# Moving one weight-load issue behind two casts on GpSimd's queue in a retention and Fourier-mixing kernel

## The chip, the cores and the metric

The kernel runs on one core of a Trainium2 chip. The metric is the device time of one execution in microseconds (us). The kernel before was run three times (233.35, 234.04 and 234.59 us), with a median of 234.04 us. One execution was recorded by the hardware profiler; it took 233.47 us, of which the profile's span covers 231.6 us.

A core has TensorE (PE, matrix products), VectorE (DVE), ScalarE (ACT), GpSimd (POOL) and SyncE (SP), each working through its own queue of instructions in order, and 16 DMA engines that serve all transfers. A transfer is issued by an instruction in some engine's queue. In this kernel the loads of q, k and v are issued by SyncE, those of the weights by GpSimd.

## What is computed

Four batches, eight heads, 768 positions, head width 64. First a retention layer, a recurrence over positions with one decay factor for each head:

```python
gamma = 1.0 - 2.0 ** (-5.0 - np.arange(H))
for t in range(S):
    state = gamma * state + einsum('bhd,bhe->bhde', k[:, :, t], v[:, :, t])
    y[:, :, t] = D ** -0.5 * einsum('bhd,bhde->bhe', q[:, :, t], state)
x = y.transpose(0, 2, 1, 3).reshape(B, S, H * D)
```

Then a Fourier mixing, a normalisation and a feed-forward layer of width 2048, each with the sum around it:

```python
u = x + real(fft(fft(x, axis=1), axis=2))
un = (u - mean(u)) / sqrt(var(u) + 1e-6)
out = u + maximum(un @ w_ch1, 0.0) @ w_ch2
```

## The kernel before

**Tiles.** The 768 positions are cut into six chunks of 128, the eight heads into four pairs. Within a chunk the retention is a masked product of q and k, applied to v; across chunks a state for each pair is carried forward. The Fourier transforms are products with tables of sines and cosines that the kernel makes at its start. The feed-forward layer works on blocks of 128 hidden columns.

**The first batch** has a schedule written out by hand: the string FIRST (lines 36 to 48) is a list of units, and each unit's instructions are pinned, on every engine that it uses, behind those of the unit before (the function pin, line 165). A unit's name has a kind, its indices, and behind the @ the engine (v VectorE, a ScalarE, g GpSimd). So the list sets for each engine the order of its queue; units of different engines wait for each other only where data or a buffer make them. The later batches follow a second list, LATER, in the same manner.

**The units around the change**, all of the first batch; the first index is the pair in the order of loading, 0 to 3:

- q3 (line 512): GpSimd's cast of the last pair's q to 16 bits.
- k30 and k31 (line 520, instructions at L528 and L530): cast of the last pair's k, scaled by a decay for each position, one head each, the first on ScalarE and the second on GpSimd.
- v21 and v22 (line 534, L542 and L545): cast of the third pair's v, chunks 0 to 2 on GpSimd, chunks 3 to 5 on ScalarE.
- t30, t31 (L559): TensorE's transposes of the last pair's q and k; e30, e31 (L568, L571): ScalarE's copies of them out of the accumulator memory.
- am30, am31 (L585): the products of q and k; ae.. (L599): their masks on VectorE.
- kv2 (L613): TensorE's products of k and v of the third pair, one for each chunk but the last.
- gk2 (L317): GpSimd's copy of the third pair's decay factors into one of two buffers.
- sc2 (L622): VectorE's scan over the chunks, which reads the products of kv2 and the factors of gk2 and writes the states s.
- yi20, yi21 (L635) and yx2 (L645): TensorE's two parts of the third pair's y, within the chunk and from the states; x20, x21 (L659, L662) scale and store them.
- fs.. (L806) and s... (L873): the first fold and the first Fourier products.
- w0 to w3 (w1_unit, L1363): issue of one quarter of the first FFN weight each; w4 to w7 (w2_unit, L1370) the same for the second. Such a transfer also turns the numbers from 32 to 16 bits. All eight are issued by GpSimd.

**The loads behind them.** SyncE issues all of the first batch's loads and two q loads of the second batch at the start. The next loads (load_unit, L246) wait until the seventh weight transfer (w6) has landed and until one product of the first batch's feed-forward layer (i13, L1184) is done.

Of the kernel before, what the change touches and what calls it, by code (L numbers as in the profile page):

```python
# [37 lines left out]
ts1 ta00 e01@a ta10 ta22 v00@g par@v q1 gk0@g k10@v k11@a ta12 am00 am01 fill3 ta42 ta11 k20@g  # L38
ae010@v ae001@v kv0 ae000@v ae011@v t10 sc0 t11 e10@a yi01 v10@g yi00 yx0 e11@a fill1 am10 q2
x01@a am11 ts3 ta32 ta20 x00@v ta01 fl4@g ae101@v ae100@v k21@a kv1 fill1 t20 ta21 e20@a ae111@v  # L40
yi11 t21 sc1 ae110@v yi10 fs0 fl2@g yx1 q3 s110 w0 k31@g e21@a x10@v am20 am21 x11@a fs1 ta40
v22@a s010 k30@a t30 e30@a t31 v21@g e31@a ae201@v ta30 ae200@v kv2 ae211@v yi21 ae210@v gk2@g
sc2 csn2@a w1 csn1@v am30 ae300@v ta31 yi20 yx2 v32@g x20@a ae301@v xs0@v x21@a ta41 fl3@a gk3@g
s100 am31 ae311@v s000 v31@g kv3 fs2 s101 ge10@a ae310@v w2 s001 w3 yi31 sc3 ge00@a yi30 yx3 g0
x30@a sa00 sa10 edge x31@v fs3 w4 gr0 sa11 csn0@v s011 xs2@a xs3@v w5 s111 xs1@a sa20 mean
# [1457 lines left out]
```

## Time and profile before

| what | value |
|---|---|
| median of three runs | 234.04 us |
| the profiled execution | 233.47 us |
| its span | 231.6 us |
| granted TensorE clock | 0.998 of full speed |
| bytes moved | 36.84 MB |
| weight transfers | 8, 512 KB each |
| median from issue to landing of a weight transfer | 10.8 us |

A row of the timeline has the start in us from the span's start, the time it takes, the engine, the line, the operation, output and inputs by the program's names with their shapes, and in brackets how long the engine stood idle before it and what ended that. A row of the chain of waits has start, duration and the work that the end of the program can be followed back to. In the rows of slices each digit is the busy share of one fortieth of the span (5.8 us) in tenths.

### The profile page before, as it was taken

How to read it: one execution, taken by the hardware profiler on the slowest of the kernel's cores; microseconds unless marked ns; L12 is line 12 of the kernel's file. 1: busy time of each engine (PE TensorE's matmuls, PEld its weight loads, DVE VectorE, ACT ScalarE, POOL GpSimd, SP SyncE). 2: the span in 40 equal slices, each digit the busy share in tenths (PEclk: the TensorE clock that was granted, in tenths of full speed). 3: DMA queues.
4: the chain of work that ended last, by engine and by line, in shares of the span. 5: the costliest groups of instructions: out<-in, count | busy, mean ns of one | idle time of the engine just before them, and what ended most of it. 6: DMA issues, size and time to landing. Idle time of an engine off the chain costs nothing.

```text
span 231.6 us, 6275 instructions
## 1 busy us (share of the span) xinstructions
PE 219.1 (95%) x2407; PEld 179.2 (77%) x2407; DVE 197.1 (85%) x490; ACT 149.5 (65%) x377; POOL 107.7 (46%) x184
## 2 busy tenths in 40 slices
PE   0888999999999999999999999999999999999993
PEld 0356779866675657988999989989889898888892
DVE  8699987859589999999999699999998977959293
ACT  5989858769998576776947748868517745232510
POOL 8378901756760399948104969832003333520000
PEclk9999999999999999999999999999999999999999
DMA  7999999999999999999998795866102221221202
GB/s 168 239 264 250 238 206 207 203 242 260 168 251 220 215 217 216 223 234 219 217 213 189 161 185 157 161 93 116 23 0 95 48 91 28 62 72 25 91 0 93
DMA packets 100957, 36.84 MB, mean 159 GB/s; under 512 B 91456, under 2 KB 97984, under 8 KB 100928
## 3 DMA queue, kind: packets, MB, share of 16 engines
q1 hardware_dynamic: 96704, 32.25, 68.2%
q0 software_dynamic: 4224, 4.19, 10.9%
q8 instruction: 19, 0.31, 0.6%
q14 instruction: 10, 0.08, 0.1%
HBM read 27.26 MB, written 6.29 MB: 145 GB/s over the span
## 4 chain that ended last, share of the span: by engine, by line
PE 69%; DVE 9%; POOL 6%; issue 6%; DMA 5%; SPq 2%; ACT 1%; DVEq 0%; POOLq 0%; ACTq 0%
PE psh L1259 24%; PE ps L1308 21%; PE psc L1206 4%; PE psh L1184 4%; DMA v<-in_v_dram 3%; DMA q<-in_q_dram 2%; PE wkA L712 2%; POOL kd L499 2%; DVE ht L1277 2%; PE ps L873 2%; DVE s L746 2%; PE wkY L763 1%; PE pq L1071 1%; PE pq L983 1%; SPq L261 1%
## 5 line engine op out<-in xcount | busy, mean ns | idle before, releaser
L1164 ACT ACTIVATE ht<-psh 128x256 f16<-128x256 f32 (+2 forms) x113 | 50.7, 474 | 35.4 <-PE psh L1259 30.0
L1259 PE MATMUL psh<-unT,w 128*128 128x256 f16 x576 | 66.3, 273 | 0.0
L1259 PEld LDWEIGHTS <-w 128*128 128x128 f16 x576 | 55.8, 98 | 6.4
L1308 PEld LDWEIGHTS <-ht 128*128 128x128 f16 x440 | 41.5, 98 | 5.3 <-issue 0.4
L1277 DVE TENSOR_TENSOR ht<-ht 128x512 f16<-128x512 f16 (+2 forms) x57 | 25.0, 455 | 6.9 <-ACT ht L1164 6.3
L1110 POOL TENSOR_TENSOR u<-u,x 128x256 f32<-128x256 f32 x21 | 13.4, 636 | 35.8 <-DVE u L1078 23.3
L724 POOL TENSOR_SCALAR_AFFINE_SELECT atm<-atm 128x512 f16<-128x512 f16 x25 | 16.3, 663 | 26.3 <-issue 19.3
L1308 PE MATMUL ps<-wide,ht 128*128 128x256 f16 x216 | 27.8, 272 | 0.1
L1206 PE MATMUL psc<-w,ht 128*128 128x512 f16 x96 | 23.2, 379 | 0.0
L722 ACT ACTIVATE atm<-wkA 128x256 f16<-128x256 f32 x50 | 16.2, 394 | 4.0 <-PE wkA L712 3.5
L1308 PE MATMUL ps<-w,ht 128*128 128x256 f16 x144 | 18.6, 273 | 0.0
L1161 DVE TENSOR_SCALAR ht<-psh 128x512 f16<-128x512 f32 (+2 forms) x20 | 11.4, 570 | 8.3 <-ACT ht L1164 4.2
L746 DVE SCALAR_TENSOR_TENSOR s<-s,gk,wkK 128x128 f16<-128x128 f16 x48 | 16.0, 342 | 1.8 <-ACT s L744 0.6
L1322 DVE SCALAR_TENSOR_TENSOR ob<-ps,stats,u 128x256 f32<-128x256 f32 (+2 forms) x27 | 14.8, 561 | 1.1 <-PE ps L1308 0.8
L1121 DVE BATCH_NORM_STATS2 bst<-u 128x6 f32<-128x512 f32 x21 | 14.4, 685 | 1.6 <-POOL u L1112 1.4
L1322 DVE SCALAR_TENSOR_TENSOR u<-ps,stats,u 128x256 f32<-128x256 f32 (+2 forms) x27 | 15.0, 562 | 0.3
L770 ACT ACTIVATE x<-wkY,gexp 128x384 f16<-128x384 f32 x24 | 12.8, 587 | 3.7 <-PE wkY L763 3.6
L1206 PEld LDWEIGHTS <-ht 128*128 128x128 f16 x96 | 8.9, 98 | 8.2 <-issue 0.2
L499 POOL TENSOR_SCALAR kd<-k,gexp 128x384 f16<-128x384 f32 x22 | 13.3, 614 | 2.8 <-DMA k<-in_k_dram 1.4
L1112 POOL TENSOR_TENSOR u<-u,x 128x256 f32<-128x256 f32 x21 | 14.0, 666 | 0.0
L508 POOL TENSOR_SCALAR v<-v 128x768 f16<-128x768 f32 x11 | 9.1, 832 | 10.4 <-DMA v<-in_v_dram 10.4
L712 PE MATMUL wkA<-qTz,kT 128*128 128x256 f16 x72 | 12.6, 273 | 0.2 <-DMA kT<-kd 0.2
(228 smaller groups left out, 463.6 us busy)
## 6 DMA issues: line engine op xcount, KB each, us to landing
out_dram<-ob SPq DMA_DIRECT2D x23, 256.0 KB, 2.9
k<-in_k_dram SPq DMA_DIRECT2D x14, 384.0 KB, 5.3
v<-in_v_dram SPq DMA_DIRECT2D x14, 384.0 KB, 5.9
q<-in_q_dram SPq DMA_DIRECT2D x12, 384.0 KB, 5.6
w<-in_moe_w_ch_dram POOLq DMA_DIRECT2D x8, 512.0 KB, 10.8
wide<-in_q_dram SPq DMA_DIRECT2D x4, 384.0 KB, 6.0
wide<-in_v_dram SPq DMA_DIRECT2D x2, 384.0 KB, 6.3
wide<-in_k_dram SPq DMA_DIRECT2D x2, 384.0 KB, 6.1
```

The lines of the kernel that those rows point to most:

```text
L499: nc.gpsimd.tensor_scalar(out=kd[:, :, h2, :], in0=k32[:, h2], scalar1=gkd[:, h0 + h2:h0 + h2 + 1], scalar2=1.0, op0=ALU.mult, op1=ALU.mult)
L712: nc.tensor.matmul(wk[:, c2], st["kT"][:, c, :], st["qT"][:, :, c, :], start=True, stop=True)
L722: nc.scalar.activation(dst[:, :, h2], wk[:, :, h2], AF.Copy, bias=0.0, scale=float(gam[2 * PAIR_ORDER[i] + h2] ** (-P)))
L724: nc.gpsimd.affine_select(out=dst, in_=dst, compare_op=ALU.is_ge, fill=0.0, base=0, pattern=[[0, 2], [0, 2], [1, P]], channel_multiplier=-1)
L746: nc.vector.scalar_tensor_tensor(out=s16[:, c], in0=s16[:, c - 1], scalar=gk2[:, hp:hp + 1], in1=wk[:, c - c0], op0=ALU.mult, op1=ALU.add)
L1121: nc.vector.bn_stats(bst, u[:, kb, :])
L1164: nc.scalar.activation(dst, src, AF.Relu, bias=0.0, scale=-1.0)
L1206: nc.tensor.matmul(psc_of[b, rb], ht16[:, fb, rb3 * P:(rb3 + 1) * P], w216[:, fb, :], start=(fb == 0), stop=(fb == NFB - 1))
L1259: nc.tensor.matmul(psh[:, t], w116[:, cb, fb * P:(fb + 1) * P], unT[:, cb, g * 256:(g + 1) * 256], start=(cb == 0), stop=(cb == 3))
L1277: nc.vector.tensor_tensor(out=out_, in0=x, in1=y, op=op)
L1308: nc.tensor.matmul(dst, lhsT, rhs[:, c0:c1], start=(n == 0 and (name is not None or k == 5 and m == 1)), stop=(n == 7), skip_group_check=True)
L1322: nc.vector.scalar_tensor_tensor(out=out_, in0=in_, scalar=r, in1=u_, op0=ALU.mult, op1=ALU.add)
```

## The change

One unit of the list FIRST is moved. The issue of the first quarter of the first FFN weight (w0) stood between the units q3 and k31 of GpSimd; it now stands behind v21, ahead of gk2. The units k31 and v21 come before it. All other units keep their order on their engines.

```diff
-yi11 t21 sc1 ae110@v yi10 fs0 fl2@g yx1 q3 s110 w0 k31@g e21@a x10@v am20 am21 x11@a fs1 ta40
-v22@a s010 k30@a t30 e30@a t31 v21@g e31@a ae201@v ta30 ae200@v kv2 ae211@v yi21 ae210@v gk2@g
+yi11 t21 sc1 ae110@v yi10 fs0 fl2@g yx1 q3 s110 k31@g e21@a x10@v am20 am21 x11@a fs1 ta40
+v22@a s010 k30@a t30 e30@a t31 v21@g w0 e31@a ae201@v ta30 ae200@v kv2 ae211@v yi21 ae210@v gk2@g
 sc2 csn2@a w1 csn1@v am30 ae300@v ta31 yi20 yx2 v32@g x20@a ae301@v xs0@v x21@a ta41 fl3@a gk3@g
```

## The prediction

> **What bounds the kernel now.** I read the page's totals first, then the chain of waits in order of time from 18 to 24 us (the only stretch in which GpSimd's order is changed), then the timeline of the same stretch, then the waits of TensorE and of SyncE's queue after it, and last the landings of the weight transfers.
>
> ```profile
> span 231.6 us, 6275 instructions
> PE 219.1 (95%) x2407; PEld 179.2 (77%) x2407; DVE 197.1 (85%) x490; ACT 149.5 (65%) x377; POOL 107.7 (46%) x184
> DMA  7999999999999999999998795866102221221202
> ```
>
> TensorE is busy for 95% of the span, and the DMA engines are at nine tenths or more from the second slice (5.8 us) to the 22nd (127 us). GpSimd, with 46%, is idle half the time on average, but an average says nothing of the stretch in question. There the chain runs through it:
>
> ```profile
> 18.52 0.88 POOL q16z L516
> 19.41 0.94 POOL w L1363
> 20.35 0.05 issue
> 20.40 0.60 POOL kd L530
> 21.00 0.05 issue
> 21.05 0.52 PE tq L559 x6
> ...
> 21.59 0.81 ACT kT L571
> ...
> 22.45 0.34 PE wkA L585 x6
> 22.79 0.28 PE wkY L635 x6
> 23.07 0.46 PE wkY L645 x10
> 23.53 0.62 PE ps L873 x6
> ```
>
> The issue of the first weight quarter (L1363) stands for 0.94 us between the cast of the last q and that of the last k, so it looks as if moving it would shorten the chain by 0.94 + 0.05 = 1.0 us. The timeline shows two things that the chain hides:
>
> ```profile
> 19.35 1.00 POOL L1363 DMA_DIRECT2D w<-in_moe_w_ch_dram  x1
> 19.90 1.95 DVE L599 SCALAR_TENSOR_TENSOR atm<-wkA,maskf 128x384 f16<-128x384 f32 x4
> 20.14 0.62 ACT L528 ACTIVATE kd<-wide,gexp 128x384 f16<-128x384 f32 x1 [0.16 <-DMA wide<-in_k_dram]
> 20.40 0.59 POOL L530 TENSOR_SCALAR kd<-wide,gexp 128x384 f16<-128x384 f32 x1
> 20.66 0.78 ACT L568 COPY qTz<-tq 128x768 f16<-128x768 f16 x1
> 20.97 0.50 POOL L542 TENSOR_SCALAR v<-wide 128x384 f16<-128x384 f32 x1
> 21.42 0.39 POOL L317 COPY gk<-gk 128x256 f32<-128x256 f32 x1
> 21.52 0.47 PE L613 MATMUL wkK<-v,kd 128*64 128x64 f16 x10
> 21.77 0.81 POOL L1363 DMA_DIRECT2D w<-in_moe_w_ch_dram  x1
> 22.10 0.82 DVE L622 TENSOR_TENSOR_SCAN s<-gk,wkK 128x320 f16<-128x320 f32 x1 [0.25 <-PE wkK L613]
> 23.00 0.53 PE L645 MATMUL wkY<-s,qTz 64*128 64x64 f16 x10
> 23.02 0.53 POOL L542 TENSOR_SCALAR v<-v 128x384 f16<-128x384 f32 x1 [0.45 <-DMA v<-in_v_dram]
> 23.88 0.50 POOL L542 TENSOR_SCALAR v<-v 128x384 f16<-128x384 f32 x1
> 25.03 0.47 PE L613 MATMUL wkK<-v,kd 128*64 128x64 f16 x10
> ```
>
> First, ScalarE's cast of the other head of the same k (L528) waited for the transfer until 20.14: before that no engine can cast this k, so most of the issue's time lies under a wait that is there anyway. Second, behind the two casts GpSimd has the decay copy (gk, L317), which the state scan on VectorE (L622) reads, and the scan's end releases the inter-chunk product on TensorE (L645): 22.10 + 0.82 = 22.92, product at 23.00.
>
> **The change part by part.** Nothing is added or removed; on GpSimd's queue one DMA issue is moved past two casts, and stays ahead of the decay copy. SyncE's queue is not touched, and on the weights' own queue the eight transfers keep their order.
>
> *The k cast* goes from 20.40 to no earlier than the landing, 20.14: a gain of at most 0.26 us. GpSimd now idles from 19.40 (18.52 + 0.88) to 20.14. Of the gain ScalarE lets 0.15 through, since the copy of kT (21.59) stands behind the copy of qT, which ends at 20.66 + 0.78 = 21.44.
>
> *The decay copy.* Start to start, the k cast takes 20.97 - 20.40 = 0.57 us, the v cast 21.42 - 20.97 = 0.45, the weight issue 20.40 - 19.35 = 1.05. So after: k cast 20.14, v cast 20.71, issue 21.16, decay copy 22.21, and its end (0.39 later) 22.60 instead of 21.81. How long the moved issue will take in its new place no row shows; the bounds are the issues there are:
>
> ```profile
> L1363 POOL DMA_DIRECT2D w<-in_moe_w_ch_dram x4: 750/802/996, 19.4 to 25.1; - x4
> DMA to landing us min/median/max: 8.1/8.2/9.9
> L1370 POOL DMA_DIRECT2D w<-in_moe_w_ch_dram x4: 762/774/785, 25.9 to 28.1; - x4
> DMA to landing us min/median/max: 11.7/14.4/17.1
> ```
>
> With 0.75 in place of 1.00 the copy ends at 22.35. I take the 1.00, since it belongs to this very transfer, which stays the first of its queue, and the others are later ones.
>
> *The scan* waited for the product of k and v (21.52 + 0.47 = 21.99) and started at 22.10; the decay copy had been ready for 0.29 us (21.81). After the change the copy is the last to come: the scan starts at about 22.65 (one gap of 0.05 behind 22.60), 0.55 us late, or 0.30 late with the short issue. VectorE has nothing else to do meanwhile (its masks end at 19.90 + 1.95 = 21.85), and what stands behind the scan there waits along.
>
> *TensorE's product* of the states starts 0.08 behind the scan's end: 22.65 + 0.82 + 0.08 = 23.55 instead of 23.00. Put against the chain, which has it at 23.07 behind the product before it, the loss is 0.48. Bounds: 0.25 to 0.55; I take 0.5. The 0.15 gained before it is lost in this wait.
>
> *The second weight issue and the two v casts behind it*: the issue ends at about 22.55 + 0.81 = 23.36, so the cast that waited for its transfer until 23.02 starts some 0.4 late, and the last cast ends near 24.8 instead of 24.38. Its reader, at 25.03, is itself 0.5 late: nothing. If that lag were not there, 24.8 would still be ahead of 25.03.
>
> *What is carried to the end.* From 23.53 on the chain is TensorE's own work, in written order, so a lag stays unless TensorE later waits for something that does not lag:
>
> ```profile
> PE pst L1153 <- ACT un L1025: 0.3, 1, 0.3
> PE wkA L712 <- DMA kT<-kd: 0.2, 1, 0.2
> ```
>
> That is all that it waited for between 30 and 125 us. The first wait hangs on work behind the late product and lags too; the second, on a transposing transfer, may not, and can swallow 0.2. So 0.3 to 0.5 of the 0.5 is left; I take 0.4.
>
> *The moved transfer.* It is issued 21.16 - 19.35 = 1.81 us later. The weights are consumed in a fixed order behind later work, and the next loads stand behind the seventh of them:
>
> ```profile
> SPq L246 <- DMA w<-in_moe_w_ch_dram: 21.9, 1, 21.9
> 42.84 0.37 SPq L246 DMA_DIRECT2D k<-in_k_dram  x1
> 47.02 1.16 POOL L499 TENSOR_SCALAR kd<-k,gexp 128x384 f16<-128x384 f32 x2 [0.40 <-DMA k<-in_k_dram]
> 48.49 0.67 PE tq L677 x12
> ```
>
> The issues take up to 1.0 us each, but one quarter lands 17.1 us behind its issue: the train is held by the engines that move it, not by its issues, and these are full (the row of nines). What the first quarter leaves free for 1.8 us goes to the loads in flight, which then are out of its way. I cost it at nothing; if the engines did run dry, it costs up to 1.5 (below).
>
> [...]
>
> Sum: 233.47 us for the profiled execution (span 231.6 and 1.9 around it) + 0.4 = 233.9. That execution lies 0.57 below the median of the three runs, 234.04; on the median the forecast is **234.4**.
>
> **The rivals.** *A late train, slower.* Should the weights land 1.81 us late, the next batch's loads start at 44.65 instead of 42.84, and the k cast ends at 47.02 + 1.16 + 1.81 = 49.99. Its transposes are reached at 48.49, 0.31 behind the cast's old end: TensorE is then late by 1.81 - 0.31 = 1.5 in all, 235.5 us, and up to 235.9 if that slack is not there. It decides from a lateness of 0.7 (0.31 and the lag of 0.4) on. For it: the first-layer quarters land a steady 8.1 to 8.2 us after their issue, as if by latency. Against it: the full engines and the landing 17.1 us behind its issue.
>
> *The earlier cast pays.* If the issue really leaves the chain, the gain lies between 0.26 (the k's landing) and 1.0 (the whole issue): 233.8 to 233.0. For it: the chain of waits as it stands. Against it: the wait until 20.14 and the decay copy, which loses more than the cast gains.
>
> *The lag is swallowed*, in waits that the modelled ends of matmuls hide, between 36 and 108 us, where loads and transposing transfers set much of the other engines' pace: 234.0. Against it: TensorE's waits come to only 0.5 there.
>
> **How the numbers follow.** Forecast (+0.3 to +0.5) 42%, late train 28%, earlier cast 20%, swallowed lag 10%. What a measurement can tell from no change is about 0.5%, 1.17 us, hence 232.87 and 235.21. The forecast and the swallowed lag lie within it (52%), the late train above it (28%). Of the earlier cast, 8 points lie within, and 12 I put beyond: its upper bound of 1.0 is near the border, and the three runs of before alone are 1.24 us apart. So 12% faster, 60% the same, 28% slower. The range goes from 233.0, the earlier cast's whole gain, to 235.9, the late train's whole price; the forecast's own is 234.1 to 234.6 by its unknown costs.
>
> **What would show it.** Right: in the changed profile ScalarE's cast of this k still waits for its transfer until about 20.1, GpSimd's k cast starts with it, the weight issue stands near 21.2, the scan is released by the decay copy (GpSimd, not TensorE) at 22.4 to 22.65, and the product L645 starts at 23.3 to 23.55; the first batch's later work stands 0.3 to 0.5 later, and SyncE's first load of the next batch still at about 42.8. Wrong: a k cast before 20.0; a scan still released by TensorE at 22.1; that first load beyond 43.5; or TensorE waits between 36 and 125 us that are not there now.

## The result and the profile after

The changed kernel takes 237.08 us (median of six runs, 235.76 to 238.44) against 234.30 for the kernel before beside it: a ratio of 1.0125, 95% interval 1.0082 to 1.0169, slower. The forecast was 234.4, with a range up to 235.9. A second measurement, 12 runs (e9 below), gives 235.76 and a ratio of 1.0057 (1.0026 to 1.0088). Slower both times; the size differs, and the profiles show much of the reason. The ratios leave out executions more than 1.5% above the fastest one of the same kernel.

The page of the changed kernel (237.00 us, span 235.2):

```profile
span 235.2 us, 6275 instructions
PE 220.5 (94%) x2407; PEld 180.6 (77%) x2407; DVE 197.4 (84%) x490; ACT 149.5 (64%) x377; POOL 108.7 (46%) x184
PEclk9999799999999999999999999999999999999998
```

All engines do the same work as before. The fifth digit of the last row (23.5 to 29.4 us) is new: TensorE's clock was not fully granted there. The timeline of the changed kernel around it:

```profile
20.14 0.59 POOL L530 TENSOR_SCALAR kd<-wide,gexp 128x384 f16<-128x384 f32 x1 [0.82 <-DMA wide<-in_k_dram]
21.14 1.00 POOL L1363 DMA_DIRECT2D w<-in_moe_w_ch_dram  x1
22.14 0.41 POOL L317 COPY gk<-gk 128x256 f32<-128x256 f32 x1
22.59 0.82 DVE L622 TENSOR_TENSOR_SCAN s<-gk,wkK 128x320 f16<-128x320 f32 x1 [0.84 <-PE wkA L585]
23.26 0.53 POOL L542 TENSOR_SCALAR v<-v 128x384 f16<-128x384 f32 x1
23.33 0.70 DVE L416 COPY csn<-csp 128x384 f16<-128x384 f16 x1
23.46 0.53 PE L645 MATMUL wkY<-s,qTz 64*128 64x64 f16 x10 [0.62 <-DVE s L622]
23.93 1.00 DVE L599 SCALAR_TENSOR_TENSOR atm<-wkA,maskf 128x384 f16<-128x384 f32 x2
```

Down to the product the forecast's times hold: cast 20.14, issue 21.14 (21.16 forecast), scan 22.59 (22.65), product 23.46 (23.55), 0.46 late. (The row names TensorE's masked products as the scan's releaser; they start at 22.22 and are not the scan's input, while the decay copy ends at 22.55, 0.04 ahead of it.) What stands behind the scan on VectorE was not looked at in the prediction: a copy of a table (L416) and the next masks (L599). Before the change:

```profile
22.84 0.36 DVE L416 COPY csn<-csp 128x384 f16<-128x384 f16 x1
23.09 1.01 DVE L599 SCALAR_TENSOR_TENSOR atm<-wkA,maskf 128x384 f16<-128x384 f32 x2
```

The copy took 0.36 us and takes 0.70, so the masks are 0.84 late, not 0.46. Next the same stretch in windows of 1 us, first the kernel before, then the changed one (busy time and instructions of PE, PEld, DVE, ACT and POOL, then the granted clock, the DMA engines' share and GB/s):

```profile
22.00:23.00 1.00, 0.83 (x18) 0.55 (x19) 0.90 (x2) 1.00 (x3) 0.57 (x1) 1.00 1.24 227
23.00:24.00 1.00, 1.00 (x19) 0.78 (x16) 1.00 (x3) 1.00 (x3) 0.97 (x3) 1.00 1.23 211
24.00:25.00 1.00, 1.00 (x14) 0.69 (x12) 0.78 (x4) 1.00 (x3) 1.00 (x2) 1.00 1.15 263
```

```profile
22.00:23.00 1.00, 0.63 (x13) 0.49 (x13) 0.41 (x1) 1.00 (x4) 1.00 (x3) 1.00 1.02 348
23.00:24.00 1.00, 0.54 (x11) 0.40 (x11) 1.00 (x3) 0.36 (x1) 0.98 (x3) 1.00 0.72 138
24.00:25.00 1.00, 0.79 (x9) 0.49 (x10) 1.00 (x4) 0.97 (x3) 1.00 (x3) 1.00 0.93 147
25.00:26.00 1.00, 1.00 (x11) 0.83 (x10) 0.78 (x3) 0.97 (x3) 1.00 (x2) 0.66 1.22 195
26.00:27.00 1.00, 1.00 (x14) 0.55 (x12) 0.91 (x3) 0.14 (x1) 1.00 (x4) 0.50 1.20 188
27.00:28.00 1.00, 1.00 (x9) 0.93 (x8) 0.86 (x2) 0.00 (x0) 1.00 (x3) 0.50 1.23 204
28.00:29.00 1.00, 1.00 (x14) 0.95 (x13) 0.52 (x2) 0.60 (x1) 1.00 (x2) 0.63 1.24 210
```

Two things show that the prediction did not have. Where TensorE's busy time fell to 0.63, 0.54 and 0.79, its clock is halved right after. Read as mixtures of 1.00 and 0.50, the values 0.66 and 0.63 make the half last 0.68 + 1 + 1 + 0.74 = 3.4 us. Three groups of six products of L873 take 1.08 to 1.15 us there, where one took 0.69 at 23.93; from the length and the value 0.50 the cost is, by estimate, up to half of it, 1.7 us of work. And the DMA engines are not full: at 23 to 25 us their share is 0.72 and 0.93 and they move 138 and 147 GB/s, where the share was 1.23 and 1.15 and they moved 211 and 263. The loads in flight were finished (348 GB/s just before) when the first weight quarter had hardly begun. The packet records of the two traces bear this out. Before, the first packet of a weight goes at 21.87 us, and from 24 to 26 us the loads still move 381 KB beside the weights. After, it goes at 23.08; from 23 to 25 us the loads move 99 KB in all, and the weights only 47 and 139 KB in the two windows.

The consequence of the second is seen at SyncE and at the landings (of the first weight's quarters, then of the second's; before, 8.1/8.2/9.9 and 11.7/14.4/17.1):

```profile
44.25 0.37 SPq L246 DMA_DIRECT2D k<-in_k_dram  x1
DMA to landing us min/median/max: 7.5/8.9/10.8
DMA to landing us min/median/max: 12.5/15.4/18.1
```

The next batch's loads, which wait for the seventh weight transfer, start at 44.25 instead of 42.84: the whole train of weights is 1.41 us late. The second weight's own issues start only 0.37 later (26.31 against 25.94), so most of this comes from the head of the queue. In this execution TensorE itself was later than that and did not wait for it; its chain of waits behind the half clock:

```profile
29.78 1.19 PE pq L983 x6
37.79 1.79 PE psh L1184 x32
50.85 0.67 PE tq L677 x12
```

Before the change the first two of them stood here, and the third at 48.49:

```profile
27.43 1.19 PE pq L983 x6
35.43 1.79 PE psh L1184 x32
```

All three are 2.35 or 2.36 us late, 0.84 of it from the masks and the rest from the half clock. On the way to the end another 1.2 us is added (the span is 3.6 longer), while TensorE waits for things it did not wait for before:

```profile
PE wkA L712 <- DMA qTz<-q16z: 1.1, 2, 0.6
PE ps L913 <- DVE ee L897: 0.7, 1, 0.7
```

So two theories stood. The **scan theory**: late decay copy, late scan, half clock. The **train theory**: weights 1.4 us late, and what waits for them.

### The profile page after: what moved, and what is told of

Read it like the earlier page. It is cut to its first block, busy times and chain, and to the rows that moved or that the text cites. A ratio compares the mean times of both kernels' runs of the same rounds, so it can differ in the third digit from the quotient of the medians.

```text
span 235.2 us, 6275 instructions
## 1 busy us (share of the span) xinstructions
PE 220.5 (94%) x2407; PEld 180.6 (77%) x2407; DVE 197.4 (84%) x490; ACT 149.5 (64%) x377; POOL 108.7 (46%) x184
## 4 chain that ended last, share of the span: by engine, by line
PE 70%; DVE 12%; DMA 7%; SPq 6%; ACT 1%; issue 1%; POOL 0%; DVEq 0%; ACTq 0%
PE psh L1259 23%; PE ps L1308 20%; PE psc L1206 7%; SPq L261 5%; PE psh L1184 4%; DMA qTz<-q16z 3%; PE wkA L712 3%; DMA wide<-in_k_dram 3%; PE ps L873 2%; PE pq L1071 2%; DVE eo L816 2%; DVE xab L789 2%; PE psh L1171 1%; DMA kT<-kd 1%; PE pq L983 1%
## 5 line engine op out<-in xcount | busy, mean ns | idle before, releaser
L1277 DVE TENSOR_TENSOR ht<-ht 128x512 f16<-128x512 f16 (+2 forms) x57 | 23.7, 433 | 7.1 <-ACT ht L1164 6.3
L1121 DVE BATCH_NORM_STATS2 bst<-u 128x6 f32<-128x512 f32 x21 | 14.4, 684 | 1.5 <-POOL u L1112 1.4
L508 POOL TENSOR_SCALAR v<-v 128x768 f16<-128x768 f32 x11 | 10.2, 926 | 9.3 <-DMA v<-in_v_dram 9.3
L499 POOL TENSOR_SCALAR kd<-k,gexp 128x384 f16<-128x384 f32 x22 | 12.8, 594 | 1.3 <-DMA k<-in_k_dram 1.3
## 6 DMA issues: line engine op xcount, KB each, us to landing
w<-in_moe_w_ch_dram POOLq DMA_DIRECT2D x8, 512.0 KB, 11.7
```

Of the source, the lines that this page charges most:

```text
L1121: nc.vector.bn_stats(bst, u[:, kb, :])
L1277: nc.vector.tensor_tensor(out=out_, in0=x, in1=y, op=op)
```

## The experiments

Each ratio is to the kernel before, run beside it on the same chip, with its 95% interval.

| run | edit | ratio |
|---|---|---|
| e1 | after, gk2 ahead of w0 | 1.0082 (1.0053 to 1.0111) |
| e2 | before, gk2 behind w1 | 1.0004 (0.9975 to 1.0034) |
| e3 | after, idle products in the waits | 1.0087 (1.0059 to 1.0114) |
| e4 | after, gk2 ahead of k31 | 1.0095 (1.0058 to 1.0132) |
| e5 | e4, i02 before i03 | 1.0059 (1.0031 to 1.0087) |
| e6 | e4, loads behind the sixth weight | 1.0039 (1.0010 to 1.0068) |
| e7 | e4 with both | 1.0032 (1.0003 to 1.0062) |
| e8 | before, w0 ahead of q3 | 0.9970 (0.9944 to 0.9996) |
| e9 | after, unedited | 1.0057 (1.0026 to 1.0088) |
| e10 | before, loads behind the sixth weight | 0.9973 (0.9944 to 1.0003) |
| e11 | before, i02 before i03 | 1.0032 (1.0005 to 1.0059) |
| e12 | e8 with e10 | 1.0001 (0.9968 to 1.0035) |
| e13 | after, csn1 on ScalarE | 1.0103 (1.0070 to 1.0136) |
| e14 | e13 with the idle products | 1.0056 (1.0022 to 1.0090) |

**One theory at a time.** e2 makes the scan late and leaves the weights on time; e1 and e4 leave the weights late and make the scan punctual.

```diff
e1  -... v21@g w0 e31@a ... ae210@v gk2@g
    +... v21@g e31@a ... ae210@v gk2@g w0
```


> The changed kernel, but the decay copy gk2 ahead of the moved weight issue (k31, v21, gk2, w0). The scan is then released by TensorE's product at about 21.9 us again, while the weight issue is as late as in the changed kernel or 0.4 us later. Scan theory (the late scan starves TensorE, and its clock is halved for 3.4 us): no half clock, TensorE's work behind the scan not later than before, time within 0.7 us of before (ratio 0.997 to 1.003), though the first load of the next batch stays at 44.2 us or later. Train theory (the weights land 1.4 us late and hold up the next batch): first load at 44.2 to 44.7 us and the time still 2 to 3 us above before (ratio 1.009 to 1.013).

```diff
e2  -... kv2 ae211@v yi21 ae210@v gk2@g
    -sc2 csn2@a w1 csn1@v
    +... kv2 ae211@v yi21 ae210@v
    +w1 gk2@g sc2 csn2@a csn1@v
```


> The kernel before with one edit: the decay copy gk2 behind the second weight issue, so that it ends near 22.6 us, as late as in the changed kernel, while the first weight issue stays in its old place. Scan theory: scan at 22.6, TensorE waits some 0.5 us for it, half clock in about as many executions as in the changed kernel, ratio 1.008 to 1.014. Train theory: the train is as before (first load of the next batch at 42.8 us) and only the plain lag of 0.5 us is seen, ratio 1.000 to 1.003.

```diff
e4  -... q3 s110 k31@g
    +... q3 s110 gk2@g k31@g
```


> The changed kernel with the decay copy gk2 ahead of the cast of the last k, in the 0.74 us in which GpSimd waits for that k to land. Weight issue at about 21.2 us as in the changed kernel. Scan theory: scan at 21.9 or a little earlier, no half clock, TensorE 0.1 to 0.2 us ahead of before, ratio 0.996 to 1.002. Train theory: the train 1.4 us late, ratio 1.009 to 1.013.

In e2 the scan is as late as in the changed kernel, and the first load as early as before:

```profile
22.53 0.82 DVE L622 TENSOR_TENSOR_SCAN s<-gk,wkK 128x320 f16<-128x320 f32 x1 [0.81 <-POOL gk L317]
42.92 0.37 SPq L246 DMA_DIRECT2D k<-in_k_dram  x1
PE wkY L645 <- DVE s L622: 0.5, 1, 0.5
```

Yet its time is that of before, 1.0004. A scan 0.43 us late, with TensorE's wait of 0.5 us, does not cost what was lost in the first measurement; it costs nothing that can be told, though the interval leaves room for 0.8 us. (Its profiled execution did have the half clock, mean 0.989, and a span of 233.6, 2.0 above that of before; of its other ten compared executions none was below 0.996.)

In e1 and e4 the scan starts at 21.8 and 21.9, ahead of before, the profiled clock is full, and the loss is there: 1.0082 and 1.0095. A punctual scan does not rule the low clock out: two of e1's eleven compared executions had it (0.992 and 0.993; 237.54 and 237.40 us) and three of e4's twelve (0.991 to 0.992; 237.08 to 238.35). Without them the means are 235.68 and 235.61 us against 234.13 for the kernel before, a loss of 0.7 and 0.6%. Where it comes from shows in the chain of waits, here of e1, which goes back to a weight transfer:

```profile
25.33 11.33 DMA w<-in_moe_w_ch_dram
36.66 0.05 issue
36.71 1.96 PE psh L1184 x32
PE psh L1184 <- DMA w<-in_moe_w_ch_dram: 1.3, 1, 1.3
```

TensorE stands at the feed-forward products of the first block row that need the fourth and third quarter (units i03 and i02, L1184) until a weight quarter lands at 36.66; before, they stood in the chain at 35.43. The last line, from its list of waits, has 1.3 us for this. In e4 that wait is 0.4, and the chain goes the other way:

```profile
27.53 16.09 DMA w<-in_moe_w_ch_dram
...
43.77 5.34 DMA k<-in_k_dram
49.11 0.09 issue
49.20 1.16 POOL kd L499 x2
50.37 0.05 issue
50.41 0.51 PE tq L677 x6
```

Weight landing, next batch's k, its cast, TensorE's transposes: the late-train rival of the prediction, piece by piece. Its price was put at 1.5 us; e4 and the kernel before beside it have medians of 235.39 and 234.18, 1.2 us apart.

The lateness of the train is no accident of one execution, but its size varies. In the profiled executions with the first weight issue at 21.1 to 21.5 us and the loads behind the seventh weight (the changed kernel, e1, e3, e4, e5, e9, e13, e14) the first load starts between 43.38 and 45.15; in those with that issue at 19.4 or earlier (the kernel before, e2, e8, e11) between 42.76 and 42.93. What sets the size from 0.5 to 2.3 us is open.

**The two ways of the late weights, one at a time**, on e4, with controls on the kernel before.

```diff
e5, e11  -U01@v i03 i02 TB
         +U01@v i02 i03 TB
e6, e10  -load_unit(b, i, 6, ...)
         +load_unit(b, i, 5, ...)
```


> The kernel of e4 (decay copy in the gap, weights late) with two units of the later list exchanged: the first batch's second block row reads the third quarter of the first weight before the fourth (i02 before i03), so the quarter that lands last is read 0.9 us later. Direct theory (the lateness costs because TensorE waits at the first FFN products for the weight quarter): that wait is gone and ratio to before falls from 1.0095 to 1.000-1.004. Load theory (it costs because the next batch's loads wait for the seventh weight transfer): ratio stays 1.007 to 1.011, with TensorE waiting for a cast of k near 49 us.

> The kernel of e4 with the loads of the second batch waiting for the sixth weight transfer instead of the seventh, which takes some 2.6 us off their start. Load theory: first load near 41 us, no wait for the cast of k, ratio to before 0.998 to 1.004. Direct theory: the wait of 0.4 to 1.3 us for the weight quarter near 35 us stays, ratio 1.006 to 1.010.

> The kernel of e4 with both edits of e5 and e6. If the late weights act by these two ways and no other, ratio to before 0.996 to 1.002; if there is a third way, 1.005 or more.

> The kernel before with the loads of the second batch waiting for the sixth weight transfer instead of the seventh (control for e6). If the next batch's loads are late already in the kernel before: ratio 0.995 to 0.998, and e6 gained partly by something that has nothing to do with the change. If they have slack there: 0.999 to 1.003.

> The kernel before with the third weight quarter read ahead of the fourth (control for e5). If the exchange brings only the later reading of the late quarter: 0.999 to 1.001 here, where no quarter is late. If it has a price of its own (the block read now is emptied by the other engine, in a new wait): 1.001 to 1.004.

The exchange has a price of its own: in e11, where no quarter is late, 1.0032, with this new wait of TensorE:

```profile
PE psh L1184 <- ACT ht L1164: 0.8, 1, 0.8
```

The earlier loads may bring a little without any lateness (e10, 0.9973, with an interval up to 1.0003). Against its own control, the loss is 1.0095 - 1 = 0.95 percentage points in e4, 1.0059 - 1.0032 = 0.27 in e5, and 1.0039 - 0.9973 = 0.66 in e6. Both ways stand in the traces: e6 has no wait for the cast of k and keeps one of 0.8 us for a weight quarter, e5 keeps 0.5 us for the cast and 0.2 for a quarter. How the loss divides between them is not settled: the differences have intervals of about 0.4 points each way, and three of e4's executions had the low clock, none of e5's or e6's, so a part of what fell away may be the clock's. e7 missed its mark of 1.002: it carries the exchange's own price.

**The other direction.** If a later issue costs, an earlier one may gain.

```diff
e8  -... q3 s110 w0 k31@g
    +... w0 q3 s110 k31@g
```


> The kernel before with the first weight issue moved the other way: ahead of the cast of the last q, where GpSimd waits 0.28 us anyway, so it starts near 18.3 us and the k cast begins at about 20.15 when its load lands. Train theory: weights land 0.5 to 1 us earlier than before, first load of the next batch at about 42 us, ratio 0.994 to 1.000. Scan theory: scan 0.2 us earlier, ratio 0.999 to 1.001. If only lateness beyond a slack costs, the same as before.

> The weight issue ahead of the cast of the last q (e8) together with the earlier loads of the second batch. If both gain by the same slack, as in e8 alone, 0.996 to 0.998; if they add, 0.993 to 0.996.

In e8 the issue lies under two waits of GpSimd, that ahead of the cast of the last q and that for the last k. The cast of q starts 0.57 later than before (19.09 against 18.52), that of k 0.30 earlier:

```profile
18.06 0.99 POOL L1363 DMA_DIRECT2D w<-in_moe_w_ch_dram  x1
19.09 0.84 POOL L516 TENSOR_SCALAR q16z<-wide 128x768 f16<-128x768 f32 x1
20.10 0.78 POOL L530 TENSOR_SCALAR kd<-wide,gexp 128x384 f16<-128x384 f32 x1 [0.17 <-DMA wide<-in_k_dram]
42.76 0.37 SPq L246 DMA_DIRECT2D k<-in_k_dram  x1
```

Its 0.9970 (233.76 us) is the lowest ratio, and the only one whose interval lies below 1, by a little and among 14. But with the first quarter issued 1.3 us earlier (18.06 against 19.35), the first load behind the weights starts only 0.1 us earlier (42.76 against 42.84), where 0.5 to 1 had been expected. That the train is held here by the engines that move it, as the prediction had assumed for the change, fits the kernel before, whose DMA share is 1.09 to 1.36 in each microsecond from 18 to 23 us; in e8 itself it was not shown. With the earlier loads added (e12, 1.0001, where at most 0.998 had been expected) no gain is seen; the intervals overlap, and why is open.

**Clock and copy.** e3 fills TensorE's waits, e13 takes the table copy off VectorE, e14 does both.

```diff
e3   -yi20 yx2 ... s100 am31
     +yi20 fill2 yx2 ... s100 fill1 am31
e13  -w1 csn1@v am30
     +w1 csn1@a am30
```


> The changed kernel with three idle products on TensorE added in its waits (two ahead of the inter-chunk product that waits for the scan, one ahead of the next masked products); each takes about 0.2 us and writes a buffer that nobody reads. Scan theory: the clock stays full, and of the 1.5 us that the half clock cost most is gained: ratio to before 1.003 to 1.008, with the lag of 0.5 to 0.8 us behind the scan still there. Train theory: no gain over the changed kernel, ratio 1.010 to 1.014 whatever the clock does.

> The changed kernel once more, unedited, for the share of its executions that show the half clock and for its ratio beside the controls of the same call. If the half clock is a part of the loss of its own: ratio 1.010 to 1.014, executions with a mean clock of 0.993 or less at least 1 us slower than the others. If the late weights are the whole of it: ratio 1.007 to 1.010, as with the decay copy in the gap, and the half clock costs nothing that shows.

> The changed kernel with the second table copy (csn1, L416) on ScalarE instead of VectorE. If VectorE's copy is held up by GpSimd's casts that run beside it: on ScalarE it takes 0.6 us whatever GpSimd does, and the masks that stood behind it on VectorE start at 23.4 instead of 23.9 to 24.8. If that stall is a part of the loss of its own: ratio to before 0.3 to 0.7 points lower than the changed kernel's (1.0057 to 1.0125). If the late weights set the time: 1.006 to 1.010 as with the scan on time (e4), since TensorE then only waits longer for the weight quarter.

> The kernel of e13 with the idle products of e3 in TensorE's waits. No execution with the half clock (mean clock under 0.994). If the late weights alone are left as cause: ratio 1.006 to 1.010, TensorE waiting for a weight quarter near 35 us; if the stall and the clock were what cost: 1.000 to 1.004.

With the idle products no low clock is seen: none of e3's 11 executions has a mean below 0.997, where seven of the 18 of the unedited changed kernel have one of 0.993 or less. That the products are the reason is likely, not shown: the 36 of e5 to e7 and the six of e13, without them, have none either. Its ratio of 1.0087 lies between what the two theories had expected and is no clear gain over 1.0125, since the intervals overlap; TensorE then waits for the weights (0.6 us), which its lag had hidden. In the first measurement of the changed kernel five of six executions had a mean clock of 0.989 to 0.993, with 236.18 to 238.44 us; the sixth, at 0.998, took 235.76. In e9 two of 12 (both 0.990; 237.05 and 238.15 us) had it; the others took 234.40 to 236.37. So the half clock, by this argument, accounts for much of the gap between 1.0125 and 1.0057; e9 itself came out below both ratios that had been expected for it. Of the 120 executions of the kernel before that were run beside e1 to e14 one had it (0.992). What decides whether an execution has it, no run shows.

e9's profiled execution, with the full clock, has the copy at its worst (VectorE's rows, then GpSimd's):

```profile
23.36 1.52 DVE L416 COPY csn<-csp 128x384 f16<-128x384 f16 x1
24.78 0.54 DVE L599 SCALAR_TENSOR_TENSOR atm<-wkA,maskf 128x384 f16<-128x384 f32 x1
```

```profile
23.29 0.52 POOL L542 TENSOR_SCALAR v<-v 128x384 f16<-128x384 f32 x1
23.75 0.40 POOL L317 COPY gk<-gk 128x256 f32<-128x256 f32 x1
24.12 0.50 POOL L542 TENSOR_SCALAR v<-v 128x384 f16<-128x384 f32 x1
```

A copy of 0.36 us takes 1.52 while GpSimd casts, copies and casts again beside it. TensorE's busy time in the windows from 22 to 26 us is 0.67, 0.51, 0.64 and 0.38, less than in the first profile, and yet the clock stays at 1.00. On ScalarE (e13) the stall is gone, as expected, and the masks start at 23.41:

```profile
22.46 1.09 ACT L416 COPY csn<-csp 128x384 f16<-128x384 f16 x2
23.41 1.00 DVE L599 SCALAR_TENSOR_TENSOR atm<-wkA,maskf 128x384 f16<-128x384 f32 x2
```

The time is not better for it: 1.0103, with six executions at a clock of 0.997 or more. Neither stall nor half clock is needed for the loss. e14 leaves the late weights and the late scan, and a ratio of 1.0056, in neither expected range. The wait for a weight quarter that had been expected is not in its profile: the first load starts at 43.38, only 0.54 late, and for the weights or a cast of k TensorE's list of waits has only 0.2 us (L677, for the cast).

## Why the prediction was wrong

*The cast, the decay copy, the scan, TensorE's product*: right, each within 0.1 us of its forecast. That the lag would be 0.4 to 0.5: mis-sized. It was 0.84 in the profiled execution and 1.69 in e9's (masks at 24.78 against 23.09), by the table copy queued behind the scan, which was pushed under GpSimd's casts and took 0.70 and 1.52 us instead of 0.36. The prediction had named what waits for the scan on VectorE only as "waits along".

*"The moved transfer ... I cost it at nothing"*: this is the step that failed. Its cover was named ("What the first quarter leaves free for 1.8 us goes to the loads in flight"), and there was not enough of it. The loads were through before the weights came up to speed, the engines moved 138 and 147 GB/s for two microseconds, and the train was 1.41 us late, out of 1.79 by which the issue had moved (21.14 against 19.35). The forecast checked the row of nines, an average over 5.8 us (it ends with the 21st slice, at 121.6 us, not the 22nd; nothing hangs on that), and the landing of 17.1 us, which belongs to the end of the queue. The question was when the queue would run dry at its beginning. The steady 8.1 to 8.2 us of the first quarters, put down as the evidence for the rival, pointed the right way, though not for the reason given there: by latency alone the seventh transfer, issued 0.37 late, would have landed 0.37 late.

*Consumers of the weights*: the rival followed only the seventh transfer to the next batch's loads. e1 shows the second way, products of the first batch (L1184) that wait for a quarter of the first weight; i03 reads the fourth quarter before i02 reads the third, so the quarter that lands last of the four is read first. No row of its landing had been set against that of its reader.

*The late-train rival*, at 28%, was the cause that the experiments support: late weights with the scan on time lose 0.8 to 0.95% (e1, e4; 0.6 to 0.7% without the executions at the low clock), a late scan with weights on time loses nothing that can be told (e2). *The swallowed lag*, at 10%, is what e2's time shows of a plain lag, though where it goes was not traced. *The half clock* was in no rival, and it carries the first measurement beyond the range: the one of its six executions without it took 235.76, inside.

Still open is how the loss divides within the changed kernel itself: there TensorE's lag and the lateness of the weights run side by side, and whichever is longer hides the other. Both profiled executions of it show the lag as the longer one, and shortening the lag or taking it away (e1, e4, e13) brings the wait for the weights to light instead of the time of before. So that e9's median of 235.76 lies near the rival's 235.5 is partly luck: in its profile TensorE's list of waits has none for the weights or for the next k. Where a lag goes later is open too: at the transposes (L677) TensorE is 2.36 late in the first profile, which ends 3.6 late, while e9's, with its masks 1.69 late, ends 1.0 late.

## What to carry to other kernels

An issue that looks like the head of a chain may lie under a wait that its neighbours have anyway (here that for the last k, until 20.14 us); find the wait first, then the slack of everything else that is queued behind the new place. The transfer moved later was not free here: the other transfers left the engines at a share of 0.72 and 0.93 for two microseconds, and an issue 1.79 us later made the train 1.41 us late. So look at the narrow windows just after its old start, not at an average, and set each landing against its first reader. And a wait can be followed by more than its own length: in the first profile TensorE's 0.62 us for the scan came ahead of about 3.4 us at half the clock (in e9 the same wait did not), and the table copy, 0.49 us late behind the scan, took 0.70 us beside GpSimd's cast instead of 0.36.

## What the runs showed of the hardware

*The clock.* With TensorE's busy time at 0.63, 0.54 and 0.79 in three successive microseconds and no wait longer than 0.62, the granted clock fell to 0.50 for about 3.4 us; in e9, with 0.67, 0.51, 0.64 and 0.38, it stayed at 1.00. So the busy time of these windows alone does not decide it.

*VectorE's copy under GpSimd's casts*: 0.36 us in the kernel before, where the cast began 0.18 behind it; 0.53 and 0.52 (e2, e8) where the cast had begun 0.22 and 0.23 ahead of it, 0.70 (first profile) and 1.52 us (e9) where it had begun 0.07 ahead. In e2, e8 and the first profile the copy ended 0.24 to 0.25 behind the cast, and GpSimd's next copy took 0.53 to 0.55 us instead of 0.39. In e9 the copy ended behind three GpSimd instructions (0.26 behind the last), not one. What lengthens the copy, and why more in e9 than in the first profile, no run shows.
